# Softmax inverse by tensor_reduce, the mixing's low part on GpSimd, later weights for the Strassen half, and other durations in the order

## The chip, the cores and the metric

The kernel runs on one core of a Trainium2 chip. A core has a matrix engine (TensorE, PE in the profile; PEld is its weight load), a vector engine (VectorE, DVE), a scalar engine (ScalarE, ACT), GpSimd (POOL) and a sync engine (SP), which here only issues DMAs. Each engine works through its own queue in order and waits at semaphores for the others. The metric is the device time of one execution in microseconds (us).

## The reference

Causal attention by blocks of 64 (8 batches, 8 heads, 576 positions, head size 64), then a mixer on the result: a low-rank mixing along the sequence (rank 32) that is added to its input, and a two-layer network along the channels (512 to 2048 to 512, with a ReLU), also added.

```python
def _attn_ref(q, k, v):
    scores = 1.0 / np.sqrt(D) * np.matmul(q, k.transpose(0, 1, 3, 2))
    mask = (pos // 64)[:, None] >= (pos // 64)[None, :]
    scores = np.where(mask, scores, -1000000000.0)
    attn = np.exp(scores - np.max(scores, axis=-1, keepdims=True))
    attn = attn / (np.sum(attn, axis=-1, keepdims=True) + 1e-09)
    return np.matmul(attn, v).astype(np.float32)

def _moe_ref(x, U, V, w_ch1, w_ch2):
    u = x + (x.transpose(0, 2, 1) @ U @ V).transpose(0, 2, 1)
    return (u + np.maximum(u @ w_ch1, 0.0) @ w_ch2).astype(np.float32)
```

Weights arrive as 64-bit floats in pairs of 32-bit words. The kernel makes 32-bit floats of them itself (`split64`).

## The kernel before, in words

Products keep nearly the accuracy of 32-bit floats by splitting operands in a high and a low part; a product is then three matmuls (high x high, high x low, low x high).

**Attention** goes head by head, 64 heads. For each head `split_qk` and `split_v` make the parts, `softmax` computes the scores of five row tiles (tile i has 128 rows and 128 i + 64 columns), their maxima on DVE (L1200) and the exponentials on ACT with their sums (L1211). `normalise` adds 1e-9 to the sums (L1227), inverts them (L1228) and multiplies the tiles by the inverse on POOL (L1237). `transpose` turns the tiles on PE (L1270), with a high part copied out by ACT and a low part by DVE (L1289); `apply_v` multiplies by V (L1313, L1329). The first twelve heads take plain 32-bit scores, the first ten plain 32-bit V products.

**The mixing** (`mix`) follows each pair of heads, 32 times: transposes (L1355), nine matmuls with U (L1369), a sum of the two halves on DVE (L1373), then the result is laid out in three parts for the product with V: high (L1374, ACT), low (L1375, DVE), high again (L1376, ACT), and two matmuls (L1384). The sums u go to DRAM.

**The mixer's first half of the channels** (`ffn_chunk`) works on 16 chunks of 288 positions: 96 fp16 matmuls for the first layer (L629), ReLU on ACT and the low part on DVE (L634, L637), 96 matmuls for the second (L654), and an addition on DVE (L666). A chunk can start when a batch's four pairs of heads are done.

**The second half of the channels** (`block_products`) uses Strassen's scheme with seven products per layer (L871), for eight batches, after all of the above. Its weights come in two high and low sets for each layer. In `weights`, a loaded matrix is scaled in place in the buffer `wr` (`late["whole"]`), split into halves (L735 on ACT, L736 on POOL), summed in place (L739 on POOL), and split again. The second layer's weights are loaded into the same buffer afterwards, and at last the running output of a batch.

**What sets the order.** The code doesn't issue instructions directly. `Plan.add` records tasks with an engine, an estimated duration and a priority; `Plan.issue` then plays them through with these durations and puts each task into its engine's queue when the play starts it. Attention has priority over the mixer's matmuls (priority 1e6 and up); these fill PE whenever the play finds PE with no attention task ready. `INTO` is the delay that the play adds before another engine sees a result. On the chip each queue keeps that order, whatever the real durations. `end` in `block_products` is the end of all tasks of attention.

`PB` gives the number of buffers of each of the five exponential tiles. `actx` and `ectx` are memory that attention releases. The tiles of the first half's hidden layer (`hh`, `hl`) lie in memory that the first ten heads release (`hidden`).

Of the kernel before, what the change touches and what calls it, by code (L numbers as in the profile page):

```python
# [9 lines left out]
F32 = mybir.dt.float32  # L10
# [4 lines left out]
ALU = mybir.AluOpType  # L15
# [31 lines left out]

FS = 12

PB = (1, 1, 1, 2, 2)  # L50


TAIL = {"PE": 165, "DVE": 78, "ACT": 105, "POOL": 20, "SP": 0}
INTO = {"PE": 355, "DVE": 35, "ACT": 35, "POOL": 90, "SP": 60}
NEAR, DL = 130, 3000
START = {"DVE": 5750, "ACT": 2750, "POOL": 3300, "SP": 700}
COL = 0.4555
# [189 lines left out]
def _dve(n):  # L247
    return 69 + 1.042 * n
# [13 lines left out]
def attention_then_mixer(  # L262
# [35 lines left out]
    def ring(pool, n, shape, dtype, name):  # L298
        return [buf(pool, shape, dtype, f"{name}{i}") for i in range(n)]
# [90 lines left out]
    def power(mu, n, by, sc, prio, pool):  # L390


        one, row = (take(r[0 if pool is banks_s else 1], f"{x}{pool is banks_s}") for r, x in ((one_r, "one"), (row_r, "row")))
        ba, bb = Buf(pool=pool), Buf(pool=pool)
        add(
            "DVE", 150, prio,
            lambda: nc.vector.tensor_reduce(out=one.ap, in_=mu[:, 0:n], op=ALU.max, axis=AX.X), mu.parts[:n], [one],
        )
        add(
            "PE", 230, prio,  # L400
            lambda: nc.tensor.matmul(ba[0:1, 0:P], one.ap, factor["ident"].ap, start=True, stop=True),
            [one], [ba],
        )
# [13 lines left out]

        add("DVE", 600, prio, exponent, [ba], [row])
        add(
            "PE", 60, prio,  # L420
            lambda: nc.tensor.matmul(bb[:, 0:2], factor[by][0:1, :], row[0:1, 2:4], start=True, stop=True), [row], [bb],
        )
        add("DVE", 150, prio, lambda: nc.vector.tensor_copy(sc.ap, bb[:, 0:2]), [bb], [sc])
# [127 lines left out]
    def second():  # L551

        if "b11" not in late:
            actx.close()
            wp2 = ctx.enter_context(tc.tile_pool(name="wp2", bufs=1))
            for x in "hl":
                late[f"w2{x}"] = wp2.tile([P, len(STAGES2), 1024], F16, name=f"w2{x}1")
            for x in ("b11", "b21", "b22"):
                late[x] = wp2.tile([P, FH, T], F32, name=f"h{x}")
        return late  # L560
# [117 lines left out]
    def block_products():  # L678
# [33 lines left out]
            return x  # L712

        def at(x, *i):
            return lambda: late[x][(slice(None), *i)]

        def weights(slots, by, sc):

# [31 lines left out]
            halves("s1", a22)  # L750
            halves("s4", a12)

        s1 = {x: (at("w1h", n), at("w1l", n), Buf(), Buf()) for n, (x, _) in enumerate(STAGES1)}
        load_w1(whole, lambda n: L, lambda: late["whole"])
        weights(s1, 0.5, scales[4])

# [258 lines left out]
    q2_r = ring(ap, 2, [P, S], F32R, "q2_")  # L1015
    k2_r = ring(ap, 2, [P, S], F32R, "k2_")
    raw_r = ring(ap, 2, [P, 2 * S], F32, "raw")
    ss_r = [b.split(5) for b in ring(ap, 2, [P, 5], F32, "ss")]

    pt_r = [ring(ap, PB[i], [P, P * (i + 1)], F32, f"p{i}_") for i in range(5)]  # L1020

# [36 lines left out]
    for r in vr_r:  # L1058
        nc.vector.memset(r[:, 10, :], 0.0)
    for j in range(2):  # L1060
        nc.vector.memset(ss_r[j].ap, 1.0)
    for i, r in enumerate(pt_r):
        for p in r:
            nc.vector.memset(p[:, P * i + 64 :], 0.0)
# [92 lines left out]
    def softmax(h, tiles, pr):  # L1157
# [35 lines left out]
        if h < FS:  # L1193
            add("PE", sum(1.667 * n for n in ns) / 2, pr, products, [raw], [bank])
        else:
            add("PE", _pe(*ns, m=ms), pr, products, [q1, k1, q2, k2], [bank])
        for i, at in parts:
            add(
                "DVE", _dve(P * i + 64), pr,
# [6 lines left out]
        for i, at in parts:  # L1206
            pt, rows = pt_r[i][h % PB[i]], P if i else 64

            def exponentials(i=i, at=at, pt=pt, rows=rows):
                out = pt[:rows, : P * i + 64]  # L1210
                nc.scalar.activation(  # L1211
                    out.rearrange("p (j k) -> p j k", j=2) if wide else out, view(i, at), AF.Exp,
                    bias=mx[:rows, i : i + 1], accum_out=ss[:rows, i : i + 1],
                )

            add(
                "ACT", _act(P * i + 64) + 188, pr, exponentials, [bank, *(mx.parts[i] for i in tiles)],
                [pt, ss.parts[i]],
            )

    def normalise(h, tiles, pr):
        ss, rv = ss_r[h % 2], rv_r[h % 2]
        cs = slice(min(tiles), max(tiles) + 1)

        def inverse():

            nc.vector.tensor_scalar(out=rv[:, cs], in0=ss[:, cs], scalar1=1e-9, scalar2=None, op0=ALU.add)  # L1227
            nc.vector.reciprocal(rv[:, cs], rv[:, cs])  # L1228

        add("DVE", 160, pr, inverse, [ss.parts[i] for i in tiles], [rv.parts[i] for i in tiles])  # L1230
        for i in tiles:
            rows, w = P if i else 64, P * i + 64
            pt = pt_r[i][h % PB[i]]
            x = pt[:rows, :w]
            add(
                "POOL", 250 + 0.85 * w, pr,
                lambda x=x, rows=rows, i=i: nc.gpsimd.tensor_scalar(  # L1237
                    out=x, in0=x, scalar1=rv[:rows, i : i + 1], scalar2=1.0, op0=ALU.mult, op1=ALU.mult
                ),
                [rv.parts[i], pt], [pt],  # L1240
            )
# [57 lines left out]
    def apply_v(h, g, pr):  # L1299
# [6 lines left out]
        if h < FP:  # L1306
            vr, pt = vr_r[h // 2 % 2], pw_r[s][g]

            def whole_products():
                for j in range(NK[g]):  # L1310

                    a, x = max(P * j - q0, 0), 5 * s + j
                    nc.tensor.matmul(  # L1313
                        bank[:, a:n], vr[:, x : x + 2, :], pt[:, _at(g, j)], start=(j == 0), stop=(j == NK[g] - 1)
                    )

            cost = sum(5 + 1.667 * (n - max(P * j - q0, 0)) for j in range(NK[g]))
            add("PE", cost, pr, whole_products, [vr, *pt.parts], [bank], hold=[xb])
            copy(False, n, pr, lambda: xt[me, q0:q1], lambda: bank[0:64, :n], [bank], [xb])
            return  # L1320
        vs, tmp, ph, pl = vs_r[s], take(tmp_r, "tmp"), ph_r[g], pl_r[g]
# [14 lines left out]
        add(  # L1336
            "DVE", _dve(n), pr, lambda: nc.vector.tensor_add(xt[me, q0:q1], bank[0:64, :n], tmp[0:64, :n]),
# [3 lines left out]
    def mix(p, pr):  # L1341
# [26 lines left out]
            for n, (x, j) in enumerate(parts):  # L1368
                nc.tensor.matmul(low[:64, 0:P], ust[:, j, :], x[:, j, :], start=(n == 0), stop=(n == 8))  # L1369

        add("PE", 505, pr, down, [xh, xl, *ust.parts], [bank], hold=[t3, tz, tb])
        add("ACT", _act(P), pr, lambda: nc.scalar.copy(tb.ap, low[R : 2 * R, 0:P]), [bank], [tb])
        add("DVE", _dve(P), pr, lambda: nc.vector.tensor_add(tz.ap, low[0:R, 0:P], tb.ap), [bank, tb], [tz])  # L1373
        add("ACT", _act(P, True), pr, lambda: nc.scalar.copy(t3[0:R, :], tz.ap), [tz], [t3])  # L1374
        add("DVE", _dve(P), pr, lambda: nc.vector.tensor_sub(t3[R : 2 * R, :], tz.ap, f32(t3[0:R, :])), [tz, t3], [t3], port=True)  # L1375
        add("ACT", _act(P, True), pr, lambda: nc.scalar.copy(t3[2 * R :, :], tz.ap), [tz], [t3])  # L1376
        for c in range(CPB):
            bank, a = Buf(pool=banks_a), c * T
# [1 line left out]
            to, dst = (ur_r[c][m], u_d[b][:, m, a : a + T]) if b == 0 else (ut.parts[c], None)  # L1380
            sums = to.ap if b == 0 else ut[:, a : a + T]
            add(
                "PE", _pe(T), pr,
                lambda bank=bank, a=a: nc.tensor.matmul(bank[:, :T], t3.ap, v3[:, a : a + T], start=True, stop=True),  # L1384
                [t3, v3.parts[c]], [bank], hold=[to],
            )
# [39 lines left out]
    for h in range(NH):  # L1426
# [15 lines left out]
        if h == min(WH, NH - 1):  # L1442
# [6 lines left out]
    def hidden():  # L1449
        ectx.close()  # L1450
        hp = ctx.enter_context(tc.tile_pool(name="hp", bufs=1, side="right"))
        for name, r, whole in (("hh", hh_r, ph_t), ("hl", hl_r, pl_t)):
            t = hp.tile([P, len(r), T], F16, name=name)
            for n, b in enumerate(r):
                b.ap = t[:, n, :]
            for n, b in enumerate(whole):
                b.ap = t[:, 2 * n : 2 * n + 2, :]

    early = [b for x in pw_r for y in x for b in y.parts]
    add("SP", 0, -1.0, hidden, early, hh_r + hl_r, hold=early)  # L1460

    for n in range(2):
        if n:
# [45 lines left out]
```

## Time and profile before

| | us |
|---|---|
| median of 3 runs | 1182.71 (1176.85 to 1183.09) |
| profiled execution, its own time | 1179.47 |
| its span, first to last instruction | 1177.7 |
| PE busy | 1132.6 (96%) |
| DVE busy | 991.8 (84%) |
| ACT busy | 793.4 (67%) |
| POOL busy | 510.3 (43%) |
| mean granted PE clock | 0.991 |

The share of busy time is a mean over stages. Until about 748 us attention runs, from about 105 us on with the first half's matmuls between its own; POOL has work until about 813 us, and from 845 us on only the Strassen products are left, with DVE and ACT making their operands.

### The profile page before, as it was taken

The page shows a single profiled execution, that of the slowest core. Times are in us where ns is not written, and L with a number is a line of the kernel's source. Part 1 is how long each engine was busy: PE and PEld are TensorE (multiplying, and loading weights), DVE is VectorE, ACT ScalarE, POOL GpSimd, SP SyncE. Part 2 cuts the span into 40 slices and gives each one's busy share as a digit, 9 for nine tenths or more (in the row PEclk, how much of TensorE's full clock was granted, in tenths as well). Part 3 has the DMA queues.
Part 4 walks back from the last instruction along what each step waited for, and adds up shares of the span by engine and source line. Part 5 has one row for each costly group of instructions (what it writes and reads, how often), then busy time and mean ns, then how long its engine had stood idle before and what let it go on. Part 6 is the DMA issues. An engine that isn't in the chain of part 4 may idle for free.

```text
span 1177.7 us, 25318 instructions
## 1 busy us (share of the span) xinstructions
PE 1132.6 (96%) x9044; PEld 934.5 (79%) x9044; DVE 991.8 (84%) x2155; ACT 793.4 (67%) x1936; POOL 510.3 (43%) x664
## 2 busy tenths in 40 slices
PE   9988996999989999999999999999999999999998
PEld 7766775888877787888888888877777777777777
DVE  6989999899987889898788878322599999999998
ACT  7778878788877878879888887331355455455543
POOL 5434444776777877676757674481000000000000
PEclk9999998999999999999999999999999999999999
DMA  4433553644433444534333341231113412331321
GB/s 137 147 125 113 159 164 98 179 138 134 129 98 87 108 138 127 160 95 110 101 110 107 98 112 42 72 100 55 49 40 102 122 42 81 121 102 39 103 82 41
DMA packets 75885, 122.70 MB, mean 104 GB/s; under 512 B 8944, under 2 KB 52976, under 8 KB 75760
## 3 DMA queue, kind: packets, MB, share of 16 engines
q1 hardware_dynamic: 75760, 121.09, 35.6%
q8 instruction: 71, 1.16, 0.4%
q14 instruction: 54, 0.44, 0.1%
HBM read 76.23 MB, written 29.49 MB: 90 GB/s over the span
## 4 chain that ended last, share of the span: by engine, by line
PE 70%; DVE 15%; ACT 10%; issue 3%; POOL 1%; DMA 1%; SPq 0%; ACTq 0%; DVEq 0%; POOLq 0%
PE bb L871 28%; PE bf L654 9%; PE bf L629 7%; PE ba L1270 5%; PE ba L1329 4%; DVE mx L1200 3%; ACT p L1211 3%; DVE pl L1289 3%; PE bg L629 2%; PE ba L1313 2%; PE bg L654 2%; DVE rv L1227 2%; PE bw L1182 1%; PE ba L1186 1%; PE ba L1187 1%
## 5 line engine op out<-in xcount | busy, mean ns | idle before, releaser
L1237 POOL TENSOR_SCALAR p<-p,rv 128x320 f32<-128x320 f32 (+4 forms) x320 | 175.3, 562 | 168.5 <-DVE rv L1228 97.5
L1270 PE MATMUL ba<-ident,p 128*128 128x128 f32 x768 | 125.3, 278 | 10.7 <-DVE tz L1373 4.7
L1211 ACT ACTIVATE p<-ba,mx 128x448 f32<-128x448 f32 (+3 forms) x248 | 114.7, 466 | 26.8 <-DVE mx L1200 19.7
L654 PE MATMUL bf<-hh,w2h 128*128 128x288 f16 x448 | 129.9, 290 | 1.5 <-DVE ot L666 0.9
L654 PE MATMUL bf<-hh,w2l 128*128 128x288 f16 x448 | 129.0, 288 | 0.4 <-DVE w2l L459 0.4
L654 PE MATMUL bf<-hl,w2h 128*128 128x288 f16 x448 | 128.9, 288 | 0.0
L654 PEld LDWEIGHTS <-w2h 128*128 128x128 f16 x1024 | 100.7, 98 | 28.3 <-issue 2.7
L1289 DVE TENSOR_TENSOR pl<-ba,ph 128x512 fp32r<-128x512 f32 x216 | 114.5, 550 | 10.0 <-ACT ph L1247 8.0
L871 PE MATMUL bb<-hh,w1h 128*128 128x288 f16 x448 | 118.9, 286 | 0.0
L871 PE MATMUL bb<-hh,w1l 128*128 128x288 f16 x448 | 118.9, 286 | 0.0
L871 PE MATMUL bb<-hh,w2l 128*128 128x288 f16 x448 | 118.9, 286 | 0.0
L871 PE MATMUL bb<-hh,w2h 128*128 128x288 f16 x448 | 118.9, 286 | 0.0
L629 PEld LDWEIGHTS <-w1h 128*128 128x128 f16 x1024 | 96.8, 98 | 26.3 <-issue 2.5
L1247 ACT CAST ph<-ba 128x512 fp32r<-128x512 f32 x216 | 100.6, 492 | 16.3 <-PE ba L1270 14.8
L799 ACT CAST hh<-hb 128x576 f16<-128x576 f32 x96 | 63.7, 666 | 66.7 <-DVE hb L825 46.4
L1270 PEld LDWEIGHTS ba<-ident,p 128*128 128x128 f32 x768 | 90.9, 142 | 19.6 <-issue 7.8
L871 PEld LDWEIGHTS <-w1h 128*128 128x128 f16 x896 | 87.7, 98 | 22.2
L871 PEld LDWEIGHTS <-w2h 128*128 128x128 f16 x896 | 87.7, 98 | 22.1
L1200 DVE TENSOR_REDUCE mx<-ba 128x1 f32<-128x448 f32 (+3 forms) x248 | 94.6, 406 | 4.8 <-PE ba L1187 3.0
L1329 PE MATMUL ba<-ph,vs 128*128 128x256 f32 (+3 forms) x432 | 93.8, 273 | 4.7 <-DVE ph L1296 3.7
L871 PE MATMUL bb<-hl,w2h 128*128 128x288 f16 x448 | 91.6, 286 | 0.0
L871 PE MATMUL bb<-hl,w1h 128*128 128x288 f16 x448 | 91.5, 286 | 0.0
(192 smaller groups left out, 3184.8 us busy)
## 6 DMA issues: line engine op xcount, KB each, us to landing
raw<-in_qk_dram SPq DMA_DIRECT2D x63, 288.0 KB, 3.9
st<-in_w_dram SPq DMA_DIRECT2D x32, 512.0 KB, 4.1
o_d<-ot SPq DMA_DIRECT2D x72, 144.0 KB, 1.8
vr<-in_v_dram SPq DMA_DIRECT2D x32, 320.0 KB, 3.8
ur<-u_d SPq DMA_DIRECT2D x64, 144.0 KB, 2.4
wr<-o_d SPq DMA_DIRECT2D x32, 288.0 KB, 3.1
out_dram<-wr SPq DMA_DIRECT2D x31, 288.0 KB, 2.3
ur<-u_d SPq DMA_DIRECT2D x30, 288.0 KB, 3.1
```

The lines of the kernel that those rows point to most:

```text
L629: nc.tensor.matmul(ps[:, :T], w()[wn][:, k, fs], m[k].ap, start=(i == 0), stop=(i == len(ops) - 1))
L654: nc.tensor.matmul(ps[:, :T], w()[wn][:, f, ms], hs[f][x].ap, start=(i == 0), stop=(i == len(ops) - 1))
L799: add("ACT", _act(2 * T, True), E, lambda: nc.scalar.copy(h.ap, x[0]()), [x[1]], [h])
L871: nc.tensor.matmul(bank[:, i, :T], x()[:, w(k)], p.ap[:, k, :], start=first and n == 0, stop=last and n == len(ops) - 1)
L1200: lambda i=i, at=at: nc.vector.tensor_reduce(out=mx[: P if i else 64, i : i + 1], in_=view(i, at), op=ALU.max, axis=AX.XY if wide else AX. ...
L1211: nc.scalar.activation(out.rearrange("p (j k) -> p j k", j=2) if wide else out, view(i, at), AF.Exp, bias=mx[:rows, i : i + 1], accum_out= ...
L1227: nc.vector.tensor_scalar(out=rv[:, cs], in0=ss[:, cs], scalar1=1e-9, scalar2=None, op0=ALU.add)
L1237: lambda x=x, rows=rows, i=i: nc.gpsimd.tensor_scalar(out=x, in0=x, scalar1=rv[:rows, i : i + 1], scalar2=1.0, op0=ALU.mult, op1=ALU.mult),
L1247: add("ACT", _act(n), pr, lambda: nc.scalar.copy(out(), inp()), reads, writes)
L1270: nc.tensor.transpose(out=bank[:, a : a + P], in_=pt_r[i][h % PB[i]][:, j * P : (j + 1) * P], identity=perm.ap)
L1289: "DVE", _dve(m), pr, lambda: nc.vector.tensor_sub(pl[:, low], bank[:, :m], f32(ph[:, low])), [bank, bh], [bl]
L1329: nc.tensor.matmul(bank[0 : c.stop, a:n], vs[:, j, c], x[:, _at(g, j)], start=(i == 0), stop=(i == len(ops) - 1))
```

## The change

- `normalise`: the sums get a second column that holds 1e-9, and a tensor_reduce over two columns takes the place of the tensor_scalar that added 1e-9.
- `mix`: the low part of the three-part operand (L1375) is computed on POOL, in place of DVE.
- The Strassen half's first-layer weight tiles are allocated with the second layer's, in memory that attention releases, and their halves wait for `end`. The hidden tiles `hh` and `hl` get memory of their own from the start; `hidden` and its wait go.
- `PB`: two buffers for each tile.
- Durations in the planner: matmuls of `power`, scores, V products and mixing are taken as longer (by 15 to 250 ns), the inverse as 260 in place of 160 ns, and a result for POOL as seen after 310 in place of 90 ns.

```diff
-PB = (1, 1, 1, 2, 2)
+PB = (2,2,2,2,2)
...
-INTO = {"PE": 355, "DVE": 35, "ACT": 35, "POOL": 90, "SP": 60}
+INTO = {"PE": 355, "DVE": 35, "ACT": 35, "POOL": 310, "SP": 60}
...
             actx.close()
+            ectx.close()
             wp2 = ctx.enter_context(tc.tile_pool(name="wp2", bufs=1))
             for x in "hl":
+                late[f"w1{x}"] = wp2.tile([P, len(STAGES1), 1024], F16, name=f"w1{x}1")
...
-        s1 = {x: (at("w1h", n), at("w1l", n), Buf(), Buf()) for n, (x, _) in enumerate(STAGES1)}
+        s1 = {x: (at("w1h", n), at("w1l", n), after(end), after(end)) for n, (x, _) in enumerate(STAGES1)}
...
-    ss_r = [b.split(5) for b in ring(ap, 2, [P, 5], F32, "ss")]
+    ss_r = [b.split(5) for b in ring(ap, 2, [P, 5, 2], F32, "ss")]
...
-        nc.vector.memset(ss_r[j].ap, 1.0)
+        nc.vector.memset(ss_r[j][:, :, 0], 1.0)
+        nc.vector.memset(ss_r[j][:, :, 1], 1e-9)
...
-            nc.vector.tensor_scalar(out=rv[:, cs], in0=ss[:, cs], scalar1=1e-9, scalar2=None, op0=ALU.add)
+            nc.vector.tensor_reduce(out=rv[:, cs], in_=ss[:, cs, :], op=ALU.add, axis=AX.X)
             nc.vector.reciprocal(rv[:, cs], rv[:, cs])
 
-        add("DVE", 160, pr, inverse, [ss.parts[i] for i in tiles], [rv.parts[i] for i in tiles])
+        add("DVE", 260, pr, inverse, [ss.parts[i] for i in tiles], [rv.parts[i] for i in tiles])
...
-        add("PE", cost, pr, products, [vs, *ph.parts, *pl.parts], [bank], hold=[xb, tmp])
+        add("PE", cost + 80, pr, products, [vs, *ph.parts, *pl.parts], [bank], hold=[xb, tmp])
...
-        add("DVE", _dve(P), pr, lambda: nc.vector.tensor_sub(t3[R : 2 * R, :], tz.ap, f32(t3[0:R, :])), [tz, t3], [t3], port=True)
+        add("POOL", 360, pr, lambda: nc.gpsimd.tensor_sub(t3[R : 2 * R, :], tz.ap, f32(t3[0:R, :])), [tz, t3], [t3])
...
-    for x in "hl":
-        late[f"w1{x}"] = wp.tile([P, len(STAGES1), 1024], F16, name=f"w1{x}1")
+    for name, r, whole in (("hh", hh_r, ph_t), ("hl", hl_r, pl_t)):
+        t = fp.tile([P, len(r), T], F16, name=name)
...
-    add("SP", 0, -1.0, hidden, early, hh_r + hl_r, hold=early)
```

The change numbers later lines differently: L1230 and L1231 are the inverse (L1227 and L1228 before), L1240 the normalising (L1237), L1376 and L1378 the mixing's sum and low part (L1373 and L1375), L738 and L741 the weights' low halves and sums (L736 and L739), L609 and L615 the scaled input of a chunk and its low part (L607 and L613).

How the queues change is shown at two places. The first is DVE's queue in the middle of attention, at the mixing of a pair of heads (`tz` is the sum of its two halves, `t` the three-part operand, `rv` the softmax inverse). Before:

```order
L1373 TENSOR_TENSOR tz_200<-ba_97,tb_201 32x128
L1227 TENSOR_SCALAR rv_188<-ss_165 128x2
L1228 RECIPROCAL rv_188<-rv_188 128x2
L351 SCALAR_TENSOR_TENSOR wr<-st_101,z_103 128x512
L1375 TENSOR_TENSOR t_0_199<-tz_200,t_0_199 32x128
L1200 TENSOR_REDUCE mx_186<-ba_98 128x1
```

And at the mixing of the same pair in the changed kernel:

```order
L1376 TENSOR_TENSOR tz_203<-ba_95,tb_204 32x128
L1292 TENSOR_TENSOR pl_194<-ba_98,ph_192 128x320
L351 SCALAR_TENSOR_TENSOR wr<-st_100,z_102 128x512
L1340 TENSOR_TENSOR xt_198<-ba_96,tmp_196 64x256
L1292 TENSOR_TENSOR pl_194<-ba_95,ph_192 128x256
L1230 TENSOR_REDUCE rv_191<-ss_165 128x2
L1231 RECIPROCAL rv_191<-rv_191 128x2
```

The write of `t` is gone from DVE, and the inverse's first step is a reduce. POOL's queue now holds that write, here between the normalising steps of a head (`p` are the exponential tiles, `q`, `k` and `vs` low parts for later heads):

```order
L1240 TENSOR_SCALAR p_1_175<-p_1_175,rv_191 128x576
L1240 TENSOR_SCALAR p_1_173<-p_1_173,rv_191 128x448
L1378 TENSOR_TENSOR t_0_202<-tz_203,t_0_202 32x128
L1240 TENSOR_SCALAR p_1_171<-p_1_171,rv_191 128x320
L1240 TENSOR_SCALAR p_1_169<-p_1_169,rv_191 128x192
```

It stands behind the two largest tiles of the head.

The second place is the Strassen half's weights in POOL's queue. Before, the first layer's low halves (`w1l`) stand among the normalising steps in the middle of attention:

```order
L1133 TENSOR_TENSOR k_1_161<-raw_163,k_1_180 64x576
L1155 TENSOR_TENSOR vs_183<-vr_181,vs_183 128x5x64
L736 TENSOR_TENSOR w1l_233<-wr,w1h_232 128x1024 x2
L1237 TENSOR_SCALAR p_0_171<-p_0_171,rv_187 128x576
L1237 TENSOR_SCALAR p_0_169<-p_0_169,rv_187 128x448
L1155 TENSOR_TENSOR vs_184<-vr_181,vs_184 128x5x64
L736 TENSOR_TENSOR w1l_233<-wr,w1h_232 128x1024
```

Now they stand behind the last mixing's low part, with only chunks of the first half around them (`us` and `ul` are a chunk's scaled input and its low part):

```order
L1378 TENSOR_TENSOR t_0_202<-tz_203,t_0_202 32x128
L615 TENSOR_TENSOR ul_129<-us_121,uh_125 128x288
L615 TENSOR_TENSOR ul_130<-us_122,uh_126 128x288
L609 TENSOR_SCALAR us_121<-ur_119,sc 128x288
L609 TENSOR_SCALAR us_122<-ur_119,sc 128x288
L738 TENSOR_TENSOR w1l_9269<-wr,w1h_9267 128x1024 x3
L741 TENSOR_TENSOR wr<-wr 128x1024 x2
```

All seven low halves and four sums of the first layer moved from among attention's steps to behind its end. Counted over the whole program, the first half's matmuls that stand ahead of attention's last matmul in PE's queue are 2280 before and 2052 afterwards, of 3072.

More of the change, by code (lines that the diff above doesn't have):

```diff
@@ L399, in power @@
         add(
-            "PE", 230, prio,
+            "PE", 310, prio,
             lambda: nc.tensor.matmul(ba[0:1, 0:P], one.ap, factor["ident"].ap, start=True, stop=True),
@@ L419, in power @@
         add(
-            "PE", 60, prio,
+            "PE", 310, prio,
             lambda: nc.tensor.matmul(bb[:, 0:2], factor[by][0:1, :], row[0:1, 2:4], start=True, stop=True), [row], [bb],
@@ L714, in at @@
         def at(x, *i):
-            return lambda: late[x][(slice(None), *i)]
+            return lambda: second()[x][(slice(None), *i)]
         def weights(slots, by, sc):
@@ L1195, in softmax @@
         else:
-            add("PE", _pe(*ns, m=ms), pr, products, [q1, k1, q2, k2], [bank])
+            add("PE", _pe(*ns, m=ms) + 40, pr, products, [q1, k1, q2, k2], [bank])
         for i, at in parts:
@@ L1212, in exponentials @@
                     out.rearrange("p (j k) -> p j k", j=2) if wide else out, view(i, at), AF.Exp,
-                    bias=mx[:rows, i : i + 1], accum_out=ss[:rows, i : i + 1],
+                    bias=mx[:rows, i : i + 1], accum_out=ss[:rows, i, 0:1],
                 )
@@ L1317, in apply_v @@
             cost = sum(5 + 1.667 * (n - max(P * j - q0, 0)) for j in range(NK[g]))
-            add("PE", cost, pr, whole_products, [vr, *pt.parts], [bank], hold=[xb])
+            add("PE", cost + 15, pr, whole_products, [vr, *pt.parts], [bank], hold=[xb])
             copy(False, n, pr, lambda: xt[me, q0:q1], lambda: bank[0:64, :n], [bank], [xb])
@@ L1369, in down @@
                 nc.tensor.matmul(low[:64, 0:P], ust[:, j, :], x[:, j, :], start=(n == 0), stop=(n == 8))
-        add("PE", 505, pr, down, [xh, xl, *ust.parts], [bank], hold=[t3, tz, tb])
+        add("PE", 590, pr, down, [xh, xl, *ust.parts], [bank], hold=[t3, tz, tb])
         add("ACT", _act(P), pr, lambda: nc.scalar.copy(tb.ap, low[R : 2 * R, 0:P]), [bank], [tb])
@@ L1382, in mix @@
             add(
-                "PE", _pe(T), pr,
+                "PE", _pe(T) + 80, pr,
                 lambda bank=bank, a=a: nc.tensor.matmul(bank[:, :T], t3.ap, v3[:, a : a + T], start=True, stop=True),
@@ L1417, in attention_then_mixer @@
     late["whole"] = wr_t[:, :, :, :].rearrange("p a (b c) n -> p a b (c n)", b=2)
-    for x in "hl":
-        late[f"w1{x}"] = wp.tile([P, len(STAGES1), 1024], F16, name=f"w1{x}1")
+    for name, r, whole in (("hh", hh_r, ph_t), ("hl", hl_r, pl_t)):
+        t = fp.tile([P, len(r), T], F16, name=name)
+        for n, b in enumerate(r):
+            b.ap = t[:, n, :]
+        for n, b in enumerate(whole):
+            b.ap = t[:, 2 * n : 2 * n + 2, :]
     wa = weight_tiles(wp, 0)
@@ L1447, in attention_then_mixer @@
             first_w2(lambda: wa, wab, lambda n: WP4 + WP3 * n, 1, [gate])
[L1449 to L1459, printed above, removed]
-    add("SP", 0, -1.0, hidden, early, hh_r + hl_r, hold=early)
     for n in range(2):
```

## The prediction

> **What bounds the kernel now.** I read the page first, then busy time by stage, then the chain of waits, then what TensorE (PE) waits for. I cut the span where the chain changes character: before the first mixer matmul (about 105 us), to the last attention matmul (748), to the first Strassen matmul (845), to the end. This is busy time by stage, with the number of instructions in brackets.
>
> ```profile
> core 0: us, PE busy (x) PEld busy (x) DVE busy (x) ACT busy (x) POOL busy (x), PEclk, DMA share, GB/s
> 0.00:105.00 105.00, 96.11 (x543) 77.42 (x544) 85.76 (x240) 82.18 (x225) 46.44 (x83) 0.98 0.44 131
> 105.00:748.00 643.00, 610.01 (x5025) 517.18 (x5024) 559.50 (x1393) 518.02 (x1405) 426.62 (x548) 0.99 0.42 118
> 748.00:845.00 97.00, 97.00 (x792) 77.03 (x790) 26.30 (x60) 26.30 (x53) 37.29 (x33) 1.00 0.25 73
> 845.00:1178.00 333.00, 329.44 (x2690) 262.91 (x2687) 320.24 (x465) 166.93 (x254) 0.00 (x0) 1.00 0.26 79
> ```
>
> PE is busy 1132.6 of 1177.7 us, so everything that an order of work can win lies in about 45 us of PE idle: 8.9 us before 105 (about 1 us of it the start), 33.0 us in the long middle stage, none from 748 to 845, about 3 us at the end. The last two stages are one chain of back-to-back matmuls:
>
> ```profile
> 833.40 11.76 PE bf L654 x96
> 845.16 329.29 PE bb L871 x2688
> ```
>
> 11.76 us / 96 = 122.5 ns for one mixer matmul. From 748 on only the amount of matmul work counts, and the change leaves that alone. The middle stage is where attention's matmuls and the mixer's (which fill PE's gaps) alternate. There VectorE (DVE) is busy for 559.5 of 643 us (87%), ScalarE (ACT) for 81%, and PE's own waits there are mostly for DVE:
>
> ```profile
> PE ba L1384 <- DVE xt L1337: 4.0, 2, 3.7
> PE ba L1270 <- DVE xt L1337: 3.9, 3, 1.8
> PE ba L1329 <- DVE ph L1296: 3.7, 3, 2.6
> PE ba L1270 <- DVE tz L1373: 2.2, 1, 2.2
> PE ba L1329 <- DVE pl L1289: 1.8, 4, 0.7
> PE ba L1270 <- ACT p L1211: 1.7, 5, 0.5
> PE ba L1270 <- DVE pl L1289: 1.7, 2, 0.9
> PE ba L1369 <- DVE xh L1360: 1.7, 2, 1.1
> PE ba L1384 <- ACT p L1211: 1.5, 2, 1.1
> PE bf L401 <- DVE onew L397: 1.2, 1, 1.2
> PE ba L1355 <- DVE xl L1360: 0.9, 2, 0.7
> ```
>
> Total, times, longest: the rows naming DVE add up to 21.1 us, in few and long waits (one of 3.7, others of 2.6 and 2.2). So DVE being late now and then costs PE two thirds of the stage's 33 us.
>
> **The change, part by part.**
>
> *Softmax inverse.* Two instructions per half head: L1227, then the reciprocal. Only the first changes. Its groups, its shortest/median/longest time, and two kinds of tensor_reduce that read SBUF:
>
> ```profile
> L1227 DVE TENSOR_SCALAR rv<-ss 128x3 f32<-128x3 f32 x64 | 21.0, 328 | 6.6 <-ACT p L1211 5.8
> L1227 DVE TENSOR_SCALAR rv<-ss 128x2 f32<-128x2 f32 x64 | 21.0, 328 | 6.6 <-ACT p L1211 5.7
> L1227 DVE TENSOR_SCALAR rv<-ss x128: 147/169/2095, 9.4 to 732.1; 128x2 f32<-128x2 f32 x64, 128x3 f32<-128x3 f32 x64
> L1401 DVE TENSOR_REDUCE um<-ut x28: 721/740/755, 120.7 to 748.3; 128x1 f32<-128x576 f32 x28
> L397 DVE TENSOR_REDUCE onew<-mu x6: 126/138/157, 50.6 to 528.6; 128x1 f32<-128x4 f32 x6
> 0.00:100.00 100.00, 3.73 (x20) 0.98 0.45 135
> ```
>
> An instruction on two or three columns that takes 147 ns at best and 2095 at worst is waiting for something else. The tensor_reduce never does: 721 to 755 ns over 28 of them, in the same stage. For 128x2x2 and 128x3x2 the nearest row is 128x4: 138 ns. So 128 x (328 - 138) = 24.3 us of DVE time goes (between 128 x (328 - 157) = 21.9 and 128 x (328 - 126) = 25.9). The last row, the inverse's windows row for the first 100 us, says where: 20 of them take 3.73 us, 187 ns each, so only about 1.0 us is won before 105 and some 23 us after.
>
> *Low part of the mixing, 32 times, from DVE to GpSimd (POOL).* The group on DVE, one case of it with what POOL did meanwhile, and POOL's nearest shapes:
>
> ```profile
> L1375 DVE TENSOR_TENSOR t<-tz,t x32: 280/316/4039, 35.8 to 745.8; 32x128 fp32r<-32x128 f32 x32
> 345.94 4.04 DVE L1375 TENSOR_TENSOR t<-tz,t 32x128 fp32r<-32x128 f32 x1 [0.36 <-ACT t L1374]
> 346.17 1.36 POOL L1237 TENSOR_SCALAR p<-p,rv 128x576 f32<-128x576 f32 x2
> 347.50 2.33 POOL L739 TENSOR_TENSOR wr<-wr 128x1024 f32<-128x1024 f32 x1
> L372 POOL TENSOR_TENSOR ust<-z,ust x2: 253/355/457, 14.2 to 15.2; 128x128 fp32r<-128x128 f32 x1, 128x32 fp32r<-128x32 f32 x1
> L372 POOL TENSOR_TENSOR v<-z,v x2: 792/802/811, 22.9 to 27.4; 32x288 fp32r<-32x288 f32 x2
> L1375 DVE TENSOR_TENSOR t<-tz,t 32x128 fp32r<-32x128 f32 x31 | 17.8, 575 | 3.0 <-ACT t L1374 2.2
> ```
>
> The DVE subtraction ran from 345.94 to 349.98, and POOL's work from 346.17 to 349.83: it ended when POOL did. Off DVE goes 32 x 0.575 = 18.4 us, 16 us of it after 105. On POOL I take 457 ns (128x128, same columns; ends 253 and 802), 14.6 us in all. For the mixing's own chain that is 0.118 us less per pair at 457, or up to 0.227 us more at 802: -4 to +7 us over 32 pairs if all of it reached PE. POOL does its queue in order, and the row of the order shows the normalising of a head ahead of this subtraction; I price the net on PE at nothing, because PE has mixer matmuls beside it, and keep both ends.
>
> A rule bears on this. The Trainium skill, page "SBUF — State Buffer", section "Who interferes with whom", says that DVE and GpSimd share one port pair as an exclusive lock, that a tensor_scalar can hold it, that a DVE instruction with two SBUF inputs waits for a GpSimd one that reads SBUF, and that tensor_reduce never contends. The rows above agree for L1227, L1375 and L1401. By that rule the moved subtraction keeps the lock and only changes sides, so it may block DVE's other two-input instructions for up to those 14.6 us, and DVE would win about 4 us instead of 18.
>
> *Weights of the Strassen half.* The w1 halves (seven casts on ACT, seven subtractions and four sums on POOL) leave the middle stage and go behind attention's end. Because they are made in the same buffer into which the second layer's weights are loaded, its eight blocks and four maxima go with them (in the order, two blocks' first two DVE steps stay early, since two staging buffers are free):
>
> ```profile
> L736 POOL TENSOR_TENSOR w1l<-wr,w1h x7: 2132/2137/2155, 332.6 to 410.2; 128x1024 f16<-128x1024 f32 x7
> L739 POOL TENSOR_TENSOR wr<-wr 128x1024 f32<-128x1024 f32 x8 | 18.9, 2360 | 0.0
> L338 DVE TENSOR_SCALAR z<-z 128x512 int32<-128x512 int32 x32 | 16.6, 522 | 0.1
> L343 DVE SCALAR_TENSOR_TENSOR z<-st,z 128x512 int32<-128x512 int32 x32 | 25.2, 789 | 0.2
> L351 DVE SCALAR_TENSOR_TENSOR wr<-st,z 128x512 int32<-128x512 int32 x32 | 26.9, 840 | 0.1
> L387 DVE TENSOR_REDUCE mu<-wr 128x1 f32<-128x1024 f32 x8 | 9.6, 1204 | 0.0
> st<-in_w_dram SPq DMA_DIRECT2D x32, 512.0 KB, 4.1
> ```
>
> POOL loses 7 x 2.137 + 4 x 2.360 = 24.4 us in the middle stage; DVE loses 6 x (0.522 + 0.789) + 8 x 0.840 + 4 x 1.204 = 19.4 us. What hides it later is the stage in which PE runs mixer matmuls alone and DVE is busy 27%. Is it long enough? The chain is 24.4 (w1 halves) + loads, two buffers at a time, four rounds of 4.1 + 2 x 2.15 = 8.4, 33.6 + 4.8 (maxima) + about 5 for the scale and the scaling + 24.4 (w2 halves) = 92 us. In the order, 1020 mixer matmuls stand behind the last attention matmul (792 before): 1020 x 0.1225 = 125 us. The w2 halves are first needed after another 168 Strassen matmuls, 20.6 us. So 146 us for 92 us: 54 us of room, part of it used by POOL's own 13 us per 97 (37.29 less the 24.4 of that stage's halves).
>
> *New durations.* They add no instruction; they decide where the mixer's matmuls stand. In the order 2280 of them stand before the last attention matmul now, 2052 afterwards: 228 x 0.1225 = 27.9 us of PE work moves from the middle stage to the tail. That is no gain by itself. It is hidden only if attention ends 27.9 us earlier; everything beyond that is gain. Their DVE part (per chunk of 192 matmuls 8 x 0.449 + 4 x 0.511) leaves the stage too:
>
> ```profile
> L637 DVE SCALAR_TENSOR_TENSOR hl<-bf,hh 128x288 f16<-128x288 f32 x96 | 43.1, 449 | 7.0 <-ACT hh L634 6.2
> L666 DVE SCALAR_TENSOR_TENSOR ot<-bf,iv,ur 128x288 f32<-128x288 f32 x54 | 27.5, 511 | 4.1 <-PE bf L654 3.2 <-PE ba L1270 0.3
> ```
>
> 5.64 us x 228 / 192 = 6.7 us. The second buffers for the three smaller exponential tiles, the added memsets and the hidden tiles' fixed place I price at nothing: the order shows the first mixer matmuls still behind the fourth mixing and ahead of the fifth, as before.
>
> *Sum.* In the middle stage DVE loses 23 + 16 + 19.4 + 6.7 = 65 of 559.5 us, 12%, and with it the 2.1 and 4.0 us outliers that make single steps late. Of the 21.1 us that PE waited for DVE I take half as gone: 10.5 us (ends: 0 and all 21.1). Before 105 DVE loses 1.0 + 1.7 us and PE idles some 8 us: 1 us. Elsewhere nothing. The profiled execution took 1179.5 us: 1179.5 - 11.5 = **1168.0 us**. The runs shown have a median of 1182.7 and a lowest of 1176.9, so the profiled one stands 3 us under the median; I keep its base.
>
> **The rivals.**
>
> *No measurable change (within 0.5%, 5.9 us, about what a measurement of this kernel can tell from none).* The order is dealt anew, and new waits take the place of the 21 us. For: PE already runs at 95% in the middle stage. Against: the long waits have a visible cause that goes. Price: 1179.5, give or take 5. The rule on the port lands here too, in a milder form: with 4 in place of 18 us of DVE time won, the same share gives about 9 us.
>
> *Slower: thin cover.* With 228 fewer matmuls between attention's steps, a head's round from scores to output, through ACT, DVE and POOL, shows on PE. If attention kept its 643 us, all 27.9 us would be added at the tail: 1179.5 + 27.9 = 1207; with half of it, 1193. It decides from the point where attention's end comes later than 748 - 28 = 720 us. For: every head has waits for the other engines. Against: they get lighter. DVE would have 559.5 - 65 = 494 us of work in 615 (80%, from 87%).
>
> *More than forecast.* All 21.1 us of DVE-named idle goes, and a good part of the 3.2 us named for ACT and of the early idle: 1179.5 - 27 = 1152.
>
> *The Strassen weights come late.* The first w2 product waits. It needs 54 us more chain than I count; 5 us of it would give 1173 with the forecast's gain.
>
> **How the numbers follow.** Forecast (1161 to 1175): 0.43. More than forecast (1145 to 1161): 0.19. No measurable change (1175 to 1187, the part under 1176.8 counted as faster): 0.23. Thin cover: 0.13. Late weights: 0.02. The range reaches from the full DVE gain with the early idle, 1150, to a third of thin cover, 1189. Faster by over 0.5% (below 1176.8): 0.43 + 0.19 + 0.02 = 0.64; within: 0.21; slower: 0.15, the thin cover and the worst of late weights.
>
> **What would show it.** Right: the inverse's first step at 130 to 160 ns with no outlier; the low part on POOL at 0.3 to 0.8 us; the last attention matmul at 705 to 712 us; after it a stage of 125 us with PE at 100% and the w1 and w2 halves inside it; DVE at about 80% in the middle stage; PE's DVE-named waits at 10 us. Wrong: attention's end later than 720, PE waits for the low part on POOL, or idle time at the first w2 product.

## The result, and the profile after

| | before | changed |
|---|---|---|
| median of 4 runs, us | 1181.43 (1176.85 to 1183.09) | 1168.86 (1168.02 to 1169.24) |
| ratio | | 0.9899, 95% interval 0.9869 to 0.9929 |
| profiled execution, us | 1179.47 | 1168.67 |
| its span, us | 1177.7 | 1166.9 |
| PE busy, us | 1132.6 | 1135.2 |
| DVE busy, us | 991.8 | 958.3 |

The changed kernel is 12.6 us faster by the medians and 10.8 us by the profiled executions; 1168.0 was predicted. Busy time by stage, cut at the same events as for the kernel before (105 us, the last attention matmul, the first Strassen matmul, the end):

```profile
0.00:105.00 105.00, 97.83 (x553) 79.03 (x554) 87.35 (x250) 80.73 (x225) 49.22 (x89) 0.98 0.48 136
105.00:708.00 603.00, 581.71 (x4781) 492.58 (x4780) 498.48 (x1304) 501.54 (x1377) 401.75 (x547) 0.99 0.42 117
708.00:834.00 126.00, 126.00 (x1025) 99.75 (x1024) 52.10 (x113) 44.99 (x82) 73.28 (x60) 1.00 0.31 94
834.00:1167.00 333.00, 329.63 (x2691) 263.06 (x2689) 320.35 (x465) 166.73 (x254) 0.00 (x0) 1.00 0.26 79
```

Attention ends at 708 in place of 748 us, and 126 us of mixer matmuls follow in place of 97: 40 us won, 29 given back. In the middle stage PE is idle for 21.3 us (603.00 - 581.71) in place of 33.0. Its busy time fell by 28.3 us, the 27.9 us of the matmuls that moved, so this stage's gain is idle time only. DVE has 498.5 us of work there, 83%. These are the largest of PE's own waits over the whole span, then the inverse's first step, the low part on POOL, and the Strassen start in the chain:

```profile
PE ba L1273 <- DVE xt L1340: 3.3, 5, 2.0
PE ba L1273 <- DVE tz L1376: 2.9, 3, 1.7
PE ba L1273 <- ACT p L1214: 2.7, 8, 0.5
PE ba L1316 <- ACT pw L1250: 2.5, 1, 2.5
PE ba L1332 <- DVE pl L1292: 1.5, 1, 1.5
L1230 DVE TENSOR_REDUCE rv<-ss x128: 129/158/160, 9.8 to 688.4; 128x2 f32<-128x4 f32 x64, 128x3 f32<-128x6 f32 x64
L1378 POOL TENSOR_TENSOR t<-tz,t x32: 445/451/1716, 32.1 to 705.3; 32x128 fp32r<-32x128 f32 x32
834.35 329.29 PE bb L873 x2688
```

The waits for `xt` of 3.7 and `ph` of 2.6 us are gone; the longest is 2.5. Added up over all rows of the middle stage, the waits that name DVE fell from 26.0 to 12.6 us, those that name ACT stayed at about 5, and none names the low part on POOL. The inverse's first step lies between 129 and 160 ns, with no outlier left.

### The profile page after: what moved, and what is told of

Read it like the earlier page. It is cut to its first block, busy times and chain, and to the rows that moved or that the text cites. A ratio compares the mean times of both kernels' runs of the same rounds, so it can differ in the third digit from the quotient of the medians.

```text
span 1166.9 us, 25406 instructions
## 1 busy us (share of the span) xinstructions
PE 1135.2 (97%) x9044; PEld 934.4 (80%) x9044; DVE 958.3 (82%) x2129; ACT 794.0 (68%) x1936; POOL 524.2 (45%) x696
## 4 chain that ended last, share of the span: by engine, by line
PE 70%; DVE 13%; ACT 12%; issue 3%; POOL 1%; DMA 0%; SPq 0%; ACTq 0%; DVEq 0%; POOLq 0%
PE bb L873 28%; PE bf L656 9%; PE bf L631 8%; PE ba L1273 5%; ACT p L1214 5%; PE ba L1332 4%; PE bg L656 3%; PE bg L631 3%; DVE mx L1203 3%; DVE pl L1292 2%; PE ba L1316 2%; PE ba L1189 1%; ACT ph L1250 1%; PE ba L1190 1%; DVE xt L1340 1%
## 5 line engine op out<-in xcount | busy, mean ns | idle before, releaser
L1240 POOL TENSOR_SCALAR p<-p,rv 128x576 f32<-128x576 f32 (+4 forms) x320 | 170.6, 548 | 125.9 <-DVE rv L1231 91.6
L1292 DVE TENSOR_TENSOR pl<-ba,ph 128x512 fp32r<-128x512 f32 x216 | 113.7, 550 | 14.8 <-ACT ph L1250 12.6
L656 PE MATMUL bf<-hh,w2h 128*128 128x288 f16 x408 | 118.2, 290 | 0.4 <-DVE ot L668 0.4
L656 PE MATMUL bf<-hl,w2h 128*128 128x288 f16 x408 | 117.3, 288 | 0.0
L656 PE MATMUL bf<-hh,w2l 128*128 128x288 f16 x408 | 117.3, 288 | 0.0
```

Of the source, the lines that this page charges most:

```text
L656: nc.tensor.matmul(ps[:, :T], w()[wn][:, f, ms], hs[f][x].ap, start=(i == 0), stop=(i == len(ops) - 1))
L1240: lambda x=x, rows=rows, i=i: nc.gpsimd.tensor_scalar(out=x, in0=x, scalar1=rv[:rows, i : i + 1], scalar2=1.0, op0=ALU.mult, op1=ALU.mult),
L1292: "DVE", _dve(m), pr, lambda: nc.vector.tensor_sub(pl[:, low], bank[:, :m], f32(ph[:, low])), [bank, bh], [bl]
```

## The experiments

All compare medians with the kernel before, run on the same chip beside them (1180.4 to 1181.7). The changed kernel's 1168.86 us was measured apart from these, and its ratio is known to about 0.3%, so a difference of two or three us from it is within the error. Where an edit touches no duration, priority or buffer count of the planner, PE's, ACT's and SP's queues keep their order exactly; that makes `a_ts`, `a_t3` and `b_inv` clean tests: one instruction differs, and the order of the other engines doesn't.

**a_ts: the inverse undone in the changed kernel.**

```diff
-            nc.vector.tensor_reduce(out=rv[:, cs], in_=ss[:, cs, :], op=ALU.add, axis=AX.X)
+            nc.vector.tensor_scalar(out=rv[:, cs], in0=ss[:, cs, 0], scalar1=1e-9, scalar2=None, op0=ALU.add)
```

> The changed kernel with the inverse's first step as a tensor_scalar again, every queue in the same order. Theory A (DVE's outliers make PE wait): the step is back to some 300 ns with outliers of 1 to 2 us, DVE gains 20 us of busy time, PE's idle time grows by 4 to 8 us and the time with it, to 1173 to 1177. Rival B (only the new order counts): DVE gains the same 20 us, but the time stays within 2 us of 1168.9.

Measured: 1181.15 us, ratio 1.0002 (0.9991 to 1.0013). This one instruction takes back the whole gain, 12.3 us. In its trace, the step and the case with the longest wait, DVE first and POOL at the same time:

```profile
L1230 DVE TENSOR_SCALAR rv<-ss x128: 140/170/2348, 9.7 to 701.9; 128x2 f32<-128x2 f32 x64, 128x3 f32<-128x3 f32 x64
435.63 2.35 DVE L1230 TENSOR_SCALAR rv<-ss 128x3 f32<-128x3 f32 x1 [0.83 <-ACT p L1214]
435.15 1.41 POOL L1135 TENSOR_TENSOR q<-raw,q 64x576 fp32r<-64x576 f32 x1
436.52 1.40 POOL L1136 TENSOR_TENSOR k<-raw,k 64x576 fp32r<-64x576 f32 x1
```

DVE's addition on three columns starts while POOL subtracts and ends at 437.98, when POOL's second subtraction (to 437.92) has ended. The reciprocal, POOL's own normalising, and everything later in DVE's queue stand behind it. It is no single case: 20 of the 128 take over 0.6 us, and each of these began while POOL worked and ended within 0.12 us of the end of a POOL instruction. By stage:

```profile
105.00:721.00 616.00, 588.65 (x4790) 495.02 (x4789) 520.56 (x1308) 503.60 (x1379) 401.38 (x547) 0.99 0.41 114
721.00:847.00 126.00, 126.00 (x1025) 99.75 (x1024) 52.01 (x112) 44.92 (x82) 73.73 (x60) 1.00 0.31 95
```

With the same PE work in the same order, attention ends 13 us later. PE's idle time in the stage grows by 6.0 us (27.3 from 21.3), all of it in waits that name DVE (18.6 from 12.6), and its busy time by 6.9. What makes the same matmuls take longer isn't shown; the ends of matmuls are modelled, so short waits could be counted as busy, and the granted clock of this profile was a little lower (0.991 against 0.993). The clock can't be the cause of the whole: among runs with a mean granted clock of 0.996, the changed kernel took 1168.0 us and `a_ts` 1179.9 to 1181.0. Rival B falls. Theory A has the mechanism, and PE's idle time within its 4 to 8 us; the time grew by more.

**b_inv: the inverse alone, in the kernel before.** The edit is the reverse of the one above, with the second column of the sums.

> The kernel before with the tensor_reduce in place of the tensor_scalar and nothing else; every queue in the order of before. Theory A (the wait for GpSimd's end inside the inverse holds DVE and then PE up, in any order): DVE loses 22 to 24 us of busy time and the kernel takes 1169 to 1175. Rival C (it is worth 12 us only in the changed order): 1178 to 1183.

Measured: 1163.08 us, ratio 0.9847 (0.9827 to 0.9866). With no other change and every queue in its old order, the kernel is 18.4 us faster than before, more than the whole change. By stage:

```profile
105.00:732.00 627.00, 606.71 (x5038) 517.21 (x5038) 538.32 (x1399) 520.35 (x1414) 426.19 (x548) 0.99 0.43 121
732.00:829.00 97.00, 97.00 (x792) 77.03 (x790) 26.30 (x61) 26.33 (x53) 37.24 (x33) 1.00 0.25 73
```

Attention ends at 732 instead of 748 us; PE idles 20.3 us in place of 33.0. PE's waits for DVE fall from 26.0 to 14.4 us, while DVE works 538 of 627 us, 86%, hardly less than the 87% before: DVE's share of busy time doesn't tell what PE waits for. Rival C falls; theory A has the mechanism, and DVE's gain of 24.8 us in all lies just above its 22 to 24, but the kernel is 6 us faster than its range.

**a_t3: the low part of the mixing on DVE again.**

```diff
-        add("POOL", 360, pr, lambda: nc.gpsimd.tensor_sub(t3[R : 2 * R, :], tz.ap, f32(t3[0:R, :])), [tz, t3], [t3])
+        add("POOL", 360, pr, lambda: nc.vector.tensor_sub(t3[R : 2 * R, :], tz.ap, f32(t3[0:R, :])), [tz, t3], [t3])
```

> The changed kernel with the low part of the mixing computed on DVE, at the place in program order where GpSimd would have been given it; PE's, ACT's and SP's queues unchanged. Theory A: DVE gains 12 to 18 us of busy time with outliers of up to 4 us, and the time grows by 2 to 5 us. Rival B: within 2 us of 1168.9, since the mixing's chain has mixer matmuls beside it on PE.

Measured: 1176.07 us, ratio 0.9955 (0.9942 to 0.9968): 7.2 us slower than the changed kernel (6.8 among runs with a mean granted clock of 0.996). The group in this trace:

```profile
L1378 DVE TENSOR_TENSOR t<-tz,t 32x128 fp32r<-32x128 f32 x32 | 15.1, 471 | 1.6 <-ACT t L1377 0.7
```

DVE is busy 974.4 us in all, 16.1 more than in the changed kernel. 15.1 of these are the subtraction itself, so while POOL does it, nothing noticeable is blocked in its place on DVE. The milder gain that the port rule would give (4 us of DVE time) isn't borne out. Rival B falls. Theory A has DVE's part, but not the size: its longest subtraction takes 1.3 us, not 4, and the time grows by 7.2 us, not 2 to 5. PE's waits for DVE in the middle stage are 17.3 us here, against 12.6.

**a_w: first-layer weights of the Strassen half made during attention again.**

```diff
-        s1 = {x: (at("w1h", n), at("w1l", n), after(end), after(end)) for n, (x, _) in enumerate(STAGES1)}
+        s1 = {x: (at("w1h", n), at("w1l", n), Buf(), Buf()) for n, (x, _) in enumerate(STAGES1)}
...
+    add("SP", 0, -1.0, hidden, early, hh_r + hl_r, hold=early)
```

> The changed kernel with the first-layer weights of the Strassen half made during attention again (and the hidden tiles in the memory that the first ten heads release). DVE's second-layer loads, 19 us, and GpSimd's 24 us go back into the middle stage. Theory A (a lighter DVE): half as much gain, 1172 to 1176. Rival B: within 2 us of 1168.9, since PE does the same work and the other engines have room.

Measured: 1170.18 us, ratio 0.9911 (0.9896 to 0.9927), 1.3 us from the changed kernel, as rival B said. The step that takes 19 us of work off DVE and 24 off POOL brings next to nothing: work that is moved is not by itself time that is won. The order is another one here, so one or two us may be the order's.

**a_dur: all the planner's durations as before, the rest changed.**

```diff
-INTO = {"PE": 355, "DVE": 35, "ACT": 35, "POOL": 310, "SP": 60}
+INTO = {"PE": 355, "DVE": 35, "ACT": 35, "POOL": 90, "SP": 60}
...
-            add("PE", _pe(*ns, m=ms) + 40, pr, products, [q1, k1, q2, k2], [bank])
+            add("PE", _pe(*ns, m=ms), pr, products, [q1, k1, q2, k2], [bank])
...
-        add("DVE", 260, pr, inverse, [ss.parts[i] for i in tiles], [rv.parts[i] for i in tiles])
+        add("DVE", 160, pr, inverse, [ss.parts[i] for i in tiles], [rv.parts[i] for i in tiles])
```

> The changed kernel with all durations of the planner as before (inverse, low part on GpSimd, later weights and second buffers kept). The order has 2082 mixer matmuls ahead of the last mixing, against 2052. Theory A: most of the gain stays, 1168 to 1173. Rival B (the durations are what shortens the stalls): 1176 to 1182.

Measured: 1155.50 us, ratio 0.9783 (0.9766 to 0.9800). Neither theory had this: the new durations cost 13.4 us.

**Which durations, and whether it is the luck of one order.** Three runs with the changed kernel's instructions: `a_into` takes back the 310 of `INTO` alone, `a_pe` the longer PE durations of scores, V products and mixing alone, and `a_deal` changes a number without meaning for this question.

```diff
-NEAR, DL = 130, 3000
+NEAR, DL = 140, 3000
```

> The changed kernel with the planner's delay for results seen by GpSimd at 90 again in place of 310, the other new durations kept; nothing that runs is different but the order. Theory D (this one delay is what the new durations cost): 1153 to 1160. Rival E (the longer PE durations are what costs, or no single one): 1165 to 1172.

> The changed kernel with the planner's PE durations for scores, V products and mixing as before (the delay for GpSimd, the inverse's 260 and the power's 310 stay new). Theory E (the longer PE durations are what the new durations cost): 1154 to 1161. Rival (no single group of durations, but their sum or the order's luck): 1163 to 1170.

> A control: the changed kernel with the planner's delay between tasks of one engine at 140 in place of 130, which deals the order anew without a meaning. If single orders scatter little, 1166 to 1172; if what the durations do to the time is the luck of one order, it can lie anywhere between 1155 and 1182.

| run | us | ratio, 95% interval |
|---|---|---|
| a_into | 1166.08 | 0.9879 (0.9860 to 0.9898) |
| a_pe | 1154.14 | 0.9776 (0.9763 to 0.9790) |
| a_deal | 1169.27 | 0.9904 (0.9886 to 0.9922) |

The PE durations are worth 14.7 us, all of the cost (theory E of `a_pe`). The delay for POOL gives 2.8 us, which the two intervals don't tell from nothing; theory D falls. The control moved 108 mixer matmuls to the other side of attention's end (1944 ahead of it, not 2052) and the time by 0.4 us, inside its narrow range. `a_durdeal`, the same control on `a_dur`, and `b_dur`, all new durations alone in the kernel before:

> A control: the kernel with the old durations (1155.5) with the planner's delay between tasks of one engine at 140 in place of 130. If the 13 us are no luck of one order: 1151 to 1161. If they are: 1162 to 1175.

> The kernel before with all new durations and nothing else (the inverse is still a tensor_scalar, the low part on DVE); 2256 mixer matmuls ahead of the last mixing, in place of 2280. If the new durations cost what they cost in the changed kernel: 1188 to 1198. If that cost belongs to the changed kernel's order alone: 1176 to 1186.

Measured: `a_durdeal` 1158.46 us, ratio 0.9809 (0.9795 to 0.9823), 3 us from `a_dur` (its runs go from 1155.6 us at a mean granted clock of 0.994 to 1163.6 at 0.988, those of `a_dur` from 1153.9 at 0.996 to 1158.1 at 0.994, so part of the 3 us may be the clock's); `b_dur` 1188.87 us, ratio 1.0068 (1.0055 to 1.0081), 8.5 us slower than before. Both lie where the cost of the durations, and not the luck of one order, puts them. So the sign belongs to the durations, in both kernels; all of them together cost 13.4 us in the changed kernel, 10.8 between the two controls and 8.5 in the kernel before, and a new order alone moved the time by at most 3 us in two trials.

**a_mir: attention's PE durations made too short by as much.**

```diff
-            add("PE", _pe(*ns, m=ms), pr, products, [q1, k1, q2, k2], [bank])
+            add("PE", _pe(*ns, m=ms) - 40, pr, products, [q1, k1, q2, k2], [bank])
...
-        add("PE", cost, pr, products, [vs, *ph.parts, *pl.parts], [bank], hold=[xb, tmp])
+        add("PE", cost - 80, pr, products, [vs, *ph.parts, *pl.parts], [bank], hold=[xb, tmp])
```

> As the kernel with the old durations (1155.5), but with attention's PE durations shortened by as much as the change had lengthened them; 2274 mixer matmuls stand ahead of the last mixing, in place of 2082. Theory F (a plan that takes PE's steps as short keeps PE behind the plan, so that its data are there when it comes): 1143 to 1154, PE's waits for DVE under 6 us. Rival G (the old durations are near the best, or it was one lucky order): 1156 to 1170.

Measured: 1155.09 us, ratio 0.9785 (0.9769 to 0.9801), no better than `a_dur`, and on the border between the two expectations. The time doesn't show what happened; the trace does. Stages from 300 to 700 us of the changed kernel and its control `a_deal`, of `a_pe` and `a_dur`, and of `a_mir` in turn (PE busy with its instructions, then PEld, DVE, ACT, POOL):

```profile
300.00:700.00 400.00, 392.75 (x3277) 335.96 (x3275) 317.32 (x860) 335.51 (x937) 274.62 (x379) 1.00 0.39 106
300.00:700.00 400.00, 393.00 (x3286) 337.12 (x3285) 316.10 (x860) 337.13 (x943) 274.01 (x379) 1.00 0.38 105
```

```profile
300.00:700.00 400.00, 396.50 (x3368) 344.55 (x3366) 317.14 (x853) 335.35 (x936) 275.18 (x383) 1.00 0.38 106
300.00:700.00 400.00, 396.75 (x3374) 345.59 (x3373) 320.69 (x860) 336.85 (x945) 278.26 (x387) 1.00 0.38 107
```

```profile
300.00:700.00 400.00, 399.11 (x3414) 348.74 (x3411) 316.80 (x860) 336.15 (x944) 279.48 (x386) 1.00 0.39 108
```

The shorter the planner believes PE's attention steps to be, the more matmuls PE gets done in the same 400 us: 3277, 3368, 3414; in `a_mir` it is idle for 0.9 us. The control has nearly the changed kernel's count. 91 more matmuls at 0.12 us each are 11 us of PE's work, of which the idle time explains 3.8; the rest lies in what the profile counts as busy, at the same granted clock of 1.00. The other engines' work is nearly the same. Theory F holds for this stretch alone: over the whole middle stage PE's waits for DVE are 9.8 us, where it had said under 6. Behind the stretch `a_mir` loses what it won. Its Strassen products start at 816.9 us, 2.8 before those of `a_pe`, and take 339.3 us to the end, where `a_pe` takes 332.7. With 2274 mixer matmuls already done, 798 are left (97.8 us) to cover the later weights, and POOL still makes second-layer halves when the Strassen products start. DVE at that place (L810 and L827 make Strassen operands), POOL, and what PE waits for:

```profile
815.54 2.78 DVE L810 SCALAR_TENSOR_TENSOR hl<-ur,sc,hh 128x576 f16<-128x576 f32 x1 [0.90 <-ACT hh L805]
818.67 2.25 DVE L827 TENSOR_TENSOR ur<-hb,ur 128x576 f32<-128x576 f32 x1
820.96 2.78 DVE L827 TENSOR_TENSOR z<-hb,ur 128x576 f32<-128x576 f32 x1
823.66 0.75 DVE L827 TENSOR_TENSOR hb<-hb 128x576 f32<-128x576 f32 x1
824.33 0.81 DVE L810 SCALAR_TENSOR_TENSOR hl<-ur,sc,hh 128x576 f16<-128x576 f32 x1
```

```profile
815.34 2.36 POOL L741 TENSOR_TENSOR wr<-wr 128x1024 f32<-128x1024 f32 x1
817.65 2.67 POOL L738 TENSOR_TENSOR w2l<-wr,w2h 128x1024 f16<-128x1024 f32 x1
820.27 2.85 POOL L741 TENSOR_TENSOR wr<-wr 128x1024 f32<-128x1024 f32 x1
```

```profile
PE bb L873 <- DVE hl L810: 4.6, 2, 3.7
```

Operands that DVE makes in 0.75 to 0.81 us once POOL is done take 2.3 to 2.8 each while POOL's sums and subtractions run, and PE, which has no mixer matmuls left, stands still for 4.6 us. The granted clock was also lower early on in this profile (0.92 from 100 to 200 us, against 0.94 in the changed kernel and 0.97 in `a_pe`), and it is the slowest of the four runs, which go from 1153.07 to 1157.91; the median doesn't tell `a_mir` from `a_pe` and `a_dur`.

**b_pb: two buffers for each exponential tile, alone.**

```diff
-PB = (1, 1, 1, 2, 2)
+PB = (2,2,2,2,2)
```

> The kernel before with two buffers for each exponential tile and nothing else. In its order 2196 mixer matmuls stand ahead of the last mixing, in place of 2280, so this step and not the durations moves most of them. As predicted (priced at nothing): 1178 to 1183. Rival (a head can run ahead of the one before it, and attention ends earlier): 1170 to 1177.

Measured: 1176.62 us, ratio 0.9960 (0.9945 to 0.9975), 4.8 us faster, and in the rival's range. The prediction had priced it at nothing.

## Why the prediction was right, and where it was not

The time, 1168.0 against 1168.9, and the way of the sum (DVE-named waits of PE) came out; its split by parts did not. The inverse and the low part were worth more than their shares, and the new durations, which were charged with nothing, cost as much as the change won. That the total came so near was luck.

- *What bounds it.* Right. The gain of the middle stage is PE's idle time, 33.0 to 21.3 us, 11.7 where 10.5 was forecast; before 105 us PE is busy 1.7 us more, where 1 was forecast. Attention's end (708 us; 705 to 712 forecast), the stage of 126 us behind it (125) and DVE's work in the middle stage (498 us; 494) agree. PE's waits for DVE are 12.6 us, where 10 were expected. The 21.1 us from which this was halved were the largest rows only; all rows together name DVE for 26.0.
- *Inverse.* The duration was right (129 to 160 ns; DVE busy 24.8 us less in `b_inv`, 24.3 forecast). Its worth was not: one share in a pool of 65 us of DVE work that together brought 10.5, while it brings 12.3 or 18.4 us by itself. The step that failed is to go from 12% less DVE work to half of PE's waits, whatever work it is. The runs show that the amount isn't what counts: `a_w` moves 19 us of it for 1.3 us of time, `a_ts` 22 us for 12.3. What fits is that a late result on a head's path counts; no run follows a single one from DVE to the end. The prediction named the outliers too, but sized nothing by them.
- *Low part.* On POOL it takes 451 ns at the median (457 forecast). The net on PE was priced at nothing, because PE has mixer matmuls beside it; undone, it costs 7.2 us, so that cover did not hide it.
- *Later weights.* The room was right in kind: in the changed kernel the last second-layer half ends 11 us before the first Strassen product, and PE doesn't wait:

```profile
821.11 2.13 POOL L738 TENSOR_TENSOR w2l<-wr,w2h 128x1024 f16<-128x1024 f32 x1 [0.38 <-ACT w2h L737]
```

  From attention's end that is 115 us (823.2 less 708), not the 92 counted. On POOL the first-layer halves and sums end 38 us after attention, where 24 were counted, the stretch of the loads takes 49 (43), the second-layer halves and sums 28 (24); in the first and the last of these POOL also has the chunks' own work, which the count left out. The rival of late weights, given 0.02, is what `a_mir` ran into, by POOL holding DVE up and not by a missing weight.
- *New durations.* The step that failed most. The prediction took them as moving work with no price of their own, and put the shift of 228 matmuls down to them. In the order, the durations alone move 24 (2256 in `b_dur`), the second buffers alone 84 (2196 in `b_pb`). And they cost 13.4 us in the changed kernel. The prediction's slower rival, thin cover, went by the number of mixer matmuls between attention's steps. That number isn't what costs: `a_deal` has 108 fewer there than the changed kernel and takes the same time, and `b_pb` has 84 fewer than the kernel before and is faster. What fits the stretches of 300 to 700 us above, with PE idle for 7.3, 3.5 and 0.9 us, is where they stand: with PE's steps taken as longer, the plan would have PE come to a step before its data more often. No run shows this step by step, so the mechanism stays argued, and why the loss is 13.4 us in one kernel and 8.5 in the other stays open.
- *Second buffers.* Priced at nothing; 4.8 us alone in the kernel before. They were not undone in the changed kernel.

The single worths don't add up to the whole (12.3 + 7.2 + 1.3 - 13.4 is 7.4, without the buffers); each was measured in one surrounding, and with a new order except in the three clean tests. The fastest versions found are `a_pe`, the change without its longer PE durations (1154.14 us, 1.3% below the changed kernel), and `a_mir` and `a_dur`, within 1.4 us of it. Shorter PE durations together with earlier weights, which `a_mir` points to, wasn't tried.

## What to carry to other kernels

A short instruction whose longest duration is ten times its shortest waits for something: look for what runs beside it, and try a form that doesn't wait, alone and in the old order, before judging by an engine's share of busy time. In a list scheduler, an estimated duration is a setting to be tried like any other: here longer ones, those of the busiest engine above all, cost 8.5 to 13.4 us, though for one of them, the nine matmuls with U, the longer number is nearer to the profile (505 and then 590 ns in the plan; 0.75 us from 342.75 to 343.50 in the kernel before). When several edits come together, undo each at a fixed order: a right total can hide one part that costs as much as another wins.

## What the hardware showed that I had not expected

The wait of a DVE instruction for POOL doesn't always end with the POOL instruction that was running. Of the 20 long additions in `a_ts`, 15 ended with the POOL instruction during which they began, some of them although POOL's next one followed without a gap; the other 5 lasted through the next one too. The case at 435.63 us lasted through the rest of one subtraction and all of the next. In the kernel before, the 4.04 us at 345.94 lasted through the last 0.24 us of POOL's subtraction for `k` (344.77 to 346.18), two normalising steps and a sum of 2.33 us. In `a_mir`, in the lines above, the two engines take turns instead: each long DVE instruction ends about 0.6 us after a POOL instruction, while POOL's next, which follows without a gap, takes 2.67 us in place of 2.13 or 2.85 in place of 2.36.

The Trainium skill, page "SBUF — State Buffer", section "Who interferes with whom", says that whoever issues first has the pair for the whole instruction. The 15 additions and `a_mir` agree; the other 5 and the case at 345.94 show DVE kept off from one POOL instruction to the next. What decides between the two isn't shown.
